# One joint region for two heads' last keys, another bank order, two store queues and new ranks in a planned attention-and-MLP kernel

## The chip, the cores and the metric

The kernel runs on one core of a Trainium2 chip. The metric is the device time of one launch in microseconds (us), lower being better. Before the change it is 1055.42 us, the median of 3 runs (1055.08 to 1056.28).

## The reference, cut to what matters

```python
q, k, v: [4, 8, 576, 64] fp32; tau: scalar
scores = (q @ k^T) / sqrt(64)
scores = where(scores >= rowmax - tau, scores, -1e9)
attn = exp(scores - rowmax); attn /= (rowsum + 1e-9)
x = (attn @ v) as [2304 tokens, 512]
h = x @ w_in;  x = (max(h, 0) + alpha * min(h, 0)) @ w_out     # d_ff = 2048
h = x @ w_in2; out = (h - tanh(h)) @ w_out2                    # d_ff = 2048
```

## The kernel before

The 2304 tokens are handled in 9 blocks of 256: two full blocks of each of the four batches (576 = 2 x 256 + 64), and one block made of the 64 left-over queries of all batches. Two heads are one attention unit, and a unit is visited in tiles of 128 queries. For a tile, TensorE forms the scores of both heads in PSUM (`multiply`, L700), VectorE takes the row maxima (`row_max`, L573) and the threshold (L576), ScalarE lifts the scores over the threshold and takes the exponential (`row_lift`, `row_exp`, L300 and L583), and VectorE the reciprocal of the sums. The first four units (`WHOLE = 4`) keep the exponentials as they are and turn them on TensorE, `turn_whole` the first 512 keys of a head and `turn_last` (L597) its last 64; copies on ScalarE or VectorE bring them into SBUF. Later units write two 16-bit pieces (`upper`, `lower`, L618) and turn them by DMA (L628). Products with the values are L739 and L742, later L679.

Every fp32 operand of the MLPs is split into a high and a low part, so one product is three matmuls. `turned_float` rounds weights as they arrive (`rebias` on ScalarE, L300 with `tw`; `three`, L367 or L369; `middle`, L372), `hi` copies (L297 or L295 inside `copy`) and `lo` subtracts (L303). The first MLP's first product is L915 (`h_pair`), its second L1140. In the second MLP, `out_products` sums seven smaller products by Strassen's scheme (`emit_seven`, L1032) for six of a block's eight pairs, and the plain product (`emit_plain`, L1039) for two of them, the last pair included. The sums lie in two PSUM tiles of two banks each, `sc0` and `sc1`. At the end of a block ScalarE copies one quarter out (`p1`), VectorE adds the rest (`total`, `both`, L1065), and the halves go to DRAM (`store`, L1085, and for the last block L1089).

The order of all this is no program text. `Plan.add` records each operation with the engines that may do it and an estimated time, its rank, what it reads and writes, and the PSUM banks and buffers it takes. `Plan.order` then walks through time: for each engine it takes, among the operations that could start first, the one of lowest rank, and among the engines the one that starts earliest after a penalty (`POOL_PEN`, `DVE_PEN`, `ACT_PEN`) where several could do it. The constants `TA`, `PA`, `PB`, `MLP_PE`, `MLP_G`, `PREP`, `XR` and the table `OFF` set the ranks. `N_WARM` operations of two matmuls on zeros (L1189), of the highest rank, fill TensorE where it has nothing else. Every engine then executes its own list strictly in that order, and DMAs stand in the lists of SyncE (SP) and ScalarE.

```python
add({"ACT": 0.49, "DVE": 0.62}, rank + OFF["H"], lambda e, j=j: bring(e, j), ...)   # ACT or DVE
t, r, i = min(((t, ops[i][1], i) for t, i in ests if t <= low + SLACK), key=lambda x: (x[1], x[2]))
key = (t + ((late_pen if ops[i][9] else pen)[e] if len(ops[i][0]) > 1 else 0), fin)
```

Of the kernel before, what the change touches and what calls it, by code (L numbers as in the profile page):

```python
# [9 lines left out]
F32 = mybir.dt.float32  # L10
# [14 lines left out]
P = 128  # L25
BLK = 256
NBLK = 9
# [17 lines left out]
TA = 69.2859  # L45
PA, PB = -14.922, 21.7041
MLP_PE = 1954.1131
MLP_G = -1037.3118
PREP = 2416.5189
# [7 lines left out]
POOL_PEN = 0.7718  # L57
# [7 lines left out]
XR = -5767.685  # L65
# [3 lines left out]
DVE_PEN = 0.5807  # L69
OFF = {"KS": -791.84, "S": -573.01, "M": -4327.05, "TH": -2173.26, "E": -1574.86, "X": -552.67, "R": -2860.41, "N": -5093.87, "NL": -258.85, "F": -1836.12, "DT": -6146.31, "T": 21.16, "H": 2659.35, "AV": -799.7, "XC": -548.69, "XH": -2968.53}  # L70
# [165 lines left out]
def attention_mlp_mlp(ctx: ExitStack, tc: tile.TileContext, kv, q0, q1, tau, w1i, w1o, alpha, w2i, w2o, out):  # L236
# [255 lines left out]
    def prep(u, rank):  # L492
# [8 lines left out]
        def load_qk(e):  # L501
            x = take(apool, raw, [P, 1024], F32, "rw", BUFS["rw"]) if u else T[raw]
            for a in range(2):
                e.dma_start(out=x[HALVES[a], :width], in_=packed_q[qb][b, h + a][HALVES[a]])
            if k == u > 0:
                load_k(e)

        def load_k(e):
            if not u:
                take(apool, raw, [P, 1024], F32, "rw", BUFS["rw"])  # L510
# [51 lines left out]
    def softmax(tile, n, slots, rank, eT, alone=False, w=False):  # L562
# [33 lines left out]
        def turn_last(e, j):  # L596
            e.transpose(hp[:D, j, :P], T["e", (tile, j)][:, 4 * P:], ident)  # L597
# [7 lines left out]
        def bring_last(e, j):  # L605
            copy(e, T[eT[eT[j][1]][0]][HALVES[j], 8 * P:], hp[:D, j, :P])
# [24 lines left out]
        for j, s in enumerate(slots):  # L631
            both = [("sc", s, t) for t in range(2)]
            k = add({"DVE": 0.69}, rank + OFF["M"], lambda e, j=j, s=s: row_max(e, j, s), [("sc", s, "s"), ROOM], [(*st, 0, j)], both,
                    takes=[] if j else [("st", st)], after=[k] if j else [])
        js = range(n)
        for a, b in [(j, j + 1) for j in js] if alone else [(0, n)]:
            add({"DVE": 0.15}, rank + OFF["TH"], lambda e, a=a, b=b: threshold(e, a, b), [*[(*st, 0, j) for j in range(a, b)], ("const", 0), ROOM],
# [7 lines left out]
        add({"DVE": 0.14}, rank + OFF["R"], guard, [*[(*st, 2, j) for j in js], ROOM], [(*st, 3)])  # L645
        add({"DVE": 0.08}, rank + OFF["R"], inverse, [ROOM], [(*st, 3)])
        k = None
        for j in js if w else ():
# [3 lines left out]
            add({"PE": 0.111}, rank + OFF["T"], lambda e, j=j: turn_last(e, j), [(*ej, 0), ("const", 2), ROOM], [("p5", j)], [("hp", 0)])  # L652
            begun[key] = add({"ACT": 0.49, "DVE": 0.62}, rank + OFF["H"], lambda e, j=j: bring(e, j), [("po", 0), ROOM], [(*key, at)], [("hp", 1)],
                             takes=[] if at else [("eT", key)], after=[begun[key]] if at else [])
        for j in js if w else ():
            key, at, _ = eT[j]
# [663 lines left out]
```

## Time and profile before

| what | value |
|---|---|
| median of 3 runs | 1055.42 us |
| the profiled execution's own time | 1052.59 us |
| span of its instructions | 1050.8 us |
| TensorE (PE) busy | 1023.7 us, 97%, 8859 matmuls |
| VectorE (DVE) busy | 772.9 us, 74% |
| ScalarE (ACT) busy | 618.4 us, 59% |
| GpSimd (POOL) busy | 74.4 us, 7% |

The span runs from the first to the last instruction on the core; the execution's own time is 1.8 us longer. The shares are means over stages that differ: until some 165 us ACT and DVE are busy about nine tenths of the time, later PE is busy nearly all the time. PE's busy time includes the 220 matmuls on zeros.

### The profile page before, as it was taken

How to read it: one execution, taken by the hardware profiler on the slowest of the kernel's cores; microseconds unless marked ns; L12 is line 12 of the kernel's file. 1: busy time of each engine (PE TensorE's matmuls, PEld its weight loads, DVE VectorE, ACT ScalarE, POOL GpSimd, SP SyncE). 2: the span in 40 equal slices, each digit the busy share in tenths (PEclk: the TensorE clock that was granted, in tenths of full speed). 3: DMA queues.
4: the chain of work that ended last, by engine and by line, in shares of the span. 5: the costliest groups of instructions: out<-in, count | busy, mean ns of one | idle time of the engine just before them, and what ended most of it. 6: DMA issues, size and time to landing. Idle time of an engine off the chain costs nothing.

```text
span 1050.8 us, 22486 instructions
## 1 busy us (share of the span) xinstructions
PE 1023.7 (97%) x8859; PEld 928.2 (88%) x8859; DVE 772.9 (74%) x1738; ACT 618.4 (59%) x1287; POOL 74.4 (7%) x101
## 2 busy tenths in 40 slices
PE   9979989999999999999999999999999999999997
PEld 7769879999999999998999888998898898899886
DVE  6998989878788778887857787674584484485465
ACT  6988888788788788887846554442312222331321
POOL 0122121001110111101100000000000000000000
PEclk9999999999999999999999999999999999999999
DMA  6678988758786557775585433200010010010000
GB/s 195 191 181 190 209 199 176 136 109 160 141 148 136 124 120 150 140 124 119 96 219 180 135 125 116 80 21 1 21 41 21 21 41 21 21 41 21 1 21 21
DMA packets 188890, 110.76 MB, mean 105 GB/s; under 512 B 158688, under 2 KB 171248, under 8 KB 188784
## 3 DMA queue, kind: packets, MB, share of 16 engines
q1 hardware_dynamic: 188480, 108.51, 44.8%
q8 instruction: 69, 1.13, 0.4%
q10 hardware_dynamic: 304, 0.82, 0.3%
q14 instruction: 37, 0.30, 0.1%
HBM read 61.58 MB, written 9.96 MB: 68 GB/s over the span
## 4 chain that ended last, share of the span: by engine, by line
PE 59%; DVE 2%; ACT 1%; DMA 1%; issue 1%; SPq 0%; DVEq 0%; ACTq 0%
PE sc L1032 13%; PE hp L915 10%; PE acc L869 6%; PE pt L915 5%; PE acc L1140 5%; PE sc L1039 5%; PE pt L869 3%; PE hp L869 3%; PE pt L679 2%; PE sc L1104 2%; PE acc L1104 2%; PE sc L700 1%; DVE st L573 1%; DMA eT<-rw 0%; ACT e L300 0%
## 5 line engine op out<-in xcount | busy, mean ns | idle before, releaser
L915 PE MATMUL hp<-x,i 128*128 128x256 f32 (+1 forms) x1584 | 230.9, 291 | 12.8 <-ACT e L300 5.6
L915 PEld LDWEIGHTS hp<-x,i 128*128 128x128 f32 x1584 | 206.1, 191 | 24.5 <-ACT e L300 6.1
L1140 PE MATMUL acc<-g,o 128*128 128x256 f32 x1232 | 165.7, 279 | 0.8 <-POOL g L303 0.8
L1140 PEld LDWEIGHTS acc<-g,o 128*128 128x128 f32 x1232 | 152.6, 188 | 4.4 <-POOL g L303 1.0
L300 ACT ACTIVATE e<-sc,st,qscale 128x576 f32<-128x576 f32 x144 | 118.0, 828 | 31.1 <-DVE st L576 18.9
L1032 PE MATMUL sc<-wp,g 128*128 128x256 f32 x756 | 135.8, 280 | 0.0
L1032 PEld LDWEIGHTS sc<-wp,g 128*128 128x128 f32 x756 | 115.8, 188 | 1.3
L618 DVE SCALAR_TENSOR_TENSOR rw<-e,st,rw 128x576 f16<-128x576 f32 x128 | 104.7, 835 | 10.3 <-ACT rw L295 9.7
L573 DVE TENSOR_REDUCE st<-sc 128x1 f32<-128x576 f32 x144 | 102.6, 750 | 13.1 <-PE sc L700 12.1
L583 ACT ACTIVATE e<-e,natau 128x576 f32<-128x576 f32 x144 | 110.9, 774 | 0.2
L1032 PE MATMUL sc<-wp,rw 128*128 128x256 f32 x378 | 106.1, 281 | 0.8 <-ACT o L295 0.8
L295 ACT ACTIVATE rw<-e,st 128x576 f16<-128x576 f32 x103 | 78.1, 771 | 18.3 <-DVE st L589 8.0
L295 ACT ACTIVATE g<-mr 128x512 fp32r<-128x512 f32 (+1 forms) x99 | 59.1, 597 | 47.8 <-PE sc L1104 16.7
L679 PE MATMUL pt<-eT,vs 128*64 128x256 f16 (+1 forms) x1584 | 73.3, 247 | 0.2 <-DMA eT<-rw 0.2
L1032 PEld LDWEIGHTS sc<-wp,rw 128*128 128x128 f32 x378 | 71.2, 188 | 2.3 <-ACT o L295 1.0
L303 DVE TENSOR_TENSOR g<-mr,g 128x512 fp32r<-128x512 f32 x80 | 55.6, 695 | 18.9 <-ACT g L295 18.4
L679 PEld LDWEIGHTS <-vs 128*64 128x64 bf16 x1584 | 65.0, 111 | 4.8 <-issue 0.4
L700 PE MATMUL sc<-kh,qh 64*128 64x320 f32 (+1 forms) x672 | 61.7, 310 | 4.4 <-ACT e L300 4.3
L869 PE MATMUL acc<-x,i 128*128 128x512 f32 x264 | 65.5, 395 | 0.0
L700 PEld LDWEIGHTS sc<-kh,qh 64*128 64x128 f32 x672 | 49.1, 185 | 13.2 <-ACT e L300 5.5
L869 PEld LDWEIGHTS acc<-x,i 128*128 128x128 f32 x264 | 48.9, 187 | 11.4
L915 PE MATMUL pt<-x,i 128*128 128x256 f32 (+1 forms) x352 | 58.0, 311 | 0.0
(246 smaller groups left out, 1707.4 us busy)
## 6 DMA issues: line engine op xcount, KB each, us to landing
vs<-in_kv_dram SPq DMA_DIRECT2D x58, 160.0 KB, 3.0
rw<-in_w1o_dram SPq DMA_DIRECT2D x16, 512.0 KB, 4.6
rw<-in_w2i_dram SPq DMA_DIRECT2D x16, 512.0 KB, 4.8
rw<-in_w2o_dram SPq DMA_DIRECT2D x16, 512.0 KB, 4.0
rw<-in_kv_dram SPq DMA_DIRECT2D x56, 144.0 KB, 3.0
rw<-in_w1i_dram SPq DMA_DIRECT2D x15, 512.0 KB, 4.8
out_dram<-o SPq DMA_DIRECT2D x16, 256.0 KB, 2.0
x1d<-o SPq DMA_DIRECT2D x14, 256.0 KB, 2.8
```

Of the source, the lines that this page charges most:

```text
L295: e.activation(out=out_, in_=in_, func=AF.Copy, **({} if scale is None else {"scale": scale}))
L300: e.activation(out=out_, in_=in_, func=AF.Prelu, alpha=alpha, **kw)
L303: e.tensor_tensor(out=out_, in0=in_, in1=hi.bitcast(F32), op=ALU.subtract)
L573: e.tensor_reduce(out=T[st][:, 0, j:j + 1], in_=x(s), axis=AX.X, op=ALU.max, negate=True)
L583: e.activation(out=w_, in_=w_, func=AF.Exp, bias=natau, scale=1.0, accum_out=T[st][:, 2, j:j + 1])
L618: e.scalar_tensor_tensor(out=x_[:, S + D:], in0=w_, scalar=r, in1=x_[:, :S], op0=ALU.mult, op1=ALU.subtract)
L679: e.matmul(po[HALVES[a]], lhsT=plane((k, a), part, c), rhs=eT(a, block), start=(i == 0), stop=(i == len(TERMS) - 1), skip_group_check=True)
L700: e.matmul(to(a, c), lhsT=x[HALVES[a], s], rhs=y[HALVES[a], c], start=(i == 0), stop=(i == len(terms) - 1))
L869: e.matmul(hq[k], lhsT=weight(1, "i", part, f // 4)[:, c, (f % 4) * P:(f % 4 + 1) * P], rhs=slots_of_x[x][:, :, c, :], start=(n0 + i == 0) ...
L915: e.matmul(hq if both_blocks else hq[:, k, :], lhsT=weight(l, "i", part, f // 4)[:, c, (f % 4) * P:(f % 4 + 1) * P], rhs=slots_of_x[x][:, ...
L1032: e.matmul(out_, lhsT=x[:, a], rhs=y[:, b], start=(begins and i == 0 and number in (1, 2, 5, 4)), stop=(n == NPAIR - 1 and i == 2), skip_g ...
L1140: e.matmul(acc[t][:, (c % 2) * BLK:(c % 2 + 1) * BLK], lhsT=w[:, c * P:(c + 1) * P], rhs=g[:, k, :], start=(f == 0 and n == 0 and c % 2 == ...
```

## The change

`turn_last` turns both heads' last keys of a tile into one region of 128 rows of PSUM (the second head by way of a 128-column transpose, the first one over its upper half), and `bring_last` brings them with one copy of 128 rows in place of two of 64. `emit_plain` and the final `both` and `store` take `sc1` ahead of `sc0`. The last block's four stores go out on two queues, two from SP and two from ACT. At the start the queries go out on SP ahead of tau, and the keys stand behind them in the plan. Some estimated times and all rank constants and two penalties have new values.

```diff
-TA = 69.2859
-PA, PB = -14.922, 21.7041
-MLP_PE = 1954.1131
-MLP_G = -1037.3118
-PREP = 2416.5189
+TA = 67.5119
+PA, PB = -68.347, 23.0966
+MLP_PE = 2066.0365
+MLP_G = -1104.8306
+PREP = 2493.5233
...
-POOL_PEN = 0.7718
+POOL_PEN = 0.5252
...
-DVE_PEN = 0.5807
+DVE_PEN = 0.5155
...
-            first = add({"ACT": 1.1}, -300, load_k, [ROOM], [(*raw, 1)], takes=[("rw", raw), ("qk", raw)], lag=3.0)
-            add({"SYNC": 2.5}, -300, load_qk, [ROOM], [raw], lag=DMA_LAG, after=[first])
+            first = add({"SYNC": 1.3}, -300, load_qk, [ROOM], [raw], takes=[("rw", raw), ("qk", raw)], lag=3.4)
+            add({"ACT": 1.1}, -300, load_k, [ROOM], [(*raw, 1)], lag=3.6, after=[first])
...
-        def turn_last(e, j):
-            e.transpose(hp[:D, j, :P], T["e", (tile, j)][:, 4 * P:], ident)
+        def turn_last(e):
+            e.transpose(hp[:, 0, :P], T["e", (tile, 1)][:, 4 * P - D:], ident)
+            e.transpose(hp[:D, 0, :P], T["e", (tile, 0)][:, 4 * P:], ident)
...
-        def bring_last(e, j):
-            copy(e, T[eT[eT[j][1]][0]][HALVES[j], 8 * P:], hp[:D, j, :P])
+        def bring_last(e):
+            copy(e, T[eT[eT[0][1]][0]][:, 8 * P:], hp[:, 0, :P])
...
-            for t in (1, 0):
+            for t in range(2):
                 for k in range(2):
                     x = 3 - 2 * t
...
-        for t in (1, 0):
+        for t in range(2):
             x = 3 - 2 * t
...
-            add({"SYNC": 1.2}, r, store, z, [("out", m, t)], lag=3.0)
+            if m < 2 * NBLK - 1:
+                add({"SYNC": 1.2}, r, store, z, [("out", m, t)], lag=3.0)
+            else:
+                add({"SYNC": 0.6}, r, lambda e, f=store: f(e, k=0), z, [("out", m, t, 0)], lag=2.0)
+                add({"ACT": 0.6}, r, lambda e, f=store: f(e, k=1), z, [("out", m, t, 1)], lag=2.0)
```

**ACT's list at the start, before** (`rw<-in_kv_dram` are the first unit's keys, `rw<-in_w1i_dram` the first piece of weights, `e<-sc` the first tile's `row_lift`):

```order
L512 DMA rw<-in_kv_dram 64x576 x2
L351 DMA rw<-in_w1i_dram 128x1024
L1183 ACT_TABLE_LOAD
L1183 ACTIVATE nalpha<-none 128x1
L300 ACTIVATE tw<-rw 128x512
L367 ACTIVATE rw<-rw 128x512
L300 ACTIVATE e<-sc_89,st,qscale 128x576
```

and now:

```order
L351 DMA rw<-in_w1i_dram 128x1024
L510 DMA rw<-in_kv_dram 64x576 x2
L1186 ACT_TABLE_LOAD
L1186 ACTIVATE nalpha<-none 128x1
L300 ACTIVATE tw<-rw 128x512 x2
L367 ACTIVATE rw<-rw 128x512
L295 ACTIVATE i_213<-tw 128x512
L300 ACTIVATE e<-sc_89,st,qscale 128x576
```

The first weights now go out ahead of the first keys, and four operations on weights stand ahead of the first tile's `row_lift` where there were two. On PE the transpose of alpha (`hp<-ident,o`) stood behind the first scores; it now stands ahead of them, with 30 matmuls on zeros before it and 8 behind it, where 36 stood ahead of the scores.

**POOL's list, its first operations behind the constants, before** (`rw<-rw` is `three`, `i`, `o`, `qh`, `last` are high or low parts):

```order
L369 TENSOR_SCALAR rw<-rw 128x512
L303 TENSOR_TENSOR o_414<-tw,o_414 128x512
L297 TENSOR_SCALAR last<-rw 64x64
L303 TENSOR_TENSOR last<-rw,last 64x64
L303 TENSOR_TENSOR qh<-rw,qh 128x256
L369 TENSOR_SCALAR rw<-rw 128x512
```

and now:

```order
L303 TENSOR_TENSOR o_390<-tw,o_390 128x512
L369 TENSOR_SCALAR rw<-rw 128x512 x2
L297 TENSOR_SCALAR o_390<-tw 128x512
L303 TENSOR_TENSOR o0b<-tw,o_390 128x512
L369 TENSOR_SCALAR rw<-rw 128x512
L303 TENSOR_TENSOR i_602<-tw,i_602 128x512
L297 TENSOR_SCALAR qh<-rw 128x256
L297 TENSOR_SCALAR last<-rw 64x64
```

More work on weights stands on POOL. Ahead of the 289th matmul of L915, where PE has 1532 matmuls behind it in either list, POOL has 49 instructions before and 78 now, DVE 355 and 321, ACT 277 and 272.

**DVE's list at the very end, before** (the last block's sums; `sc0` holds banks 0 and 1 of PSUM, `sc1` banks 2 and 3):

```order
L1065 TENSOR_TENSOR o_13522<-sc0_89,o_13522 128x256 [waits DMAHW0_49,PE_49,Activation_49]
L1065 TENSOR_TENSOR o_13521<-sc1_90,o_13522 128x256 [waits DMAHW1_49,DVE_49]
L1065 TENSOR_TENSOR o_13521<-sc1_90,o_13521 128x256 [waits DVE_49]
L1065 TENSOR_TENSOR o_13522<-sc1_90,o_13522 128x256
L1065 TENSOR_TENSOR o_13522<-sc0_89,o_13522 128x512 [waits DVE_49,PE_49]
L1065 TENSOR_TENSOR o_13521<-sc1_90,o_13521 128x512 [waits PE_49]
```

and now:

```order
L1064 TENSOR_TENSOR o_13514<-sc0_89,o_13514 128x256 [waits DMAHW0_49,Activation_49]
L1064 TENSOR_TENSOR o_13513<-sc1_90,o_13514 128x256 [waits DMAHW1_49,DVE_49,PE_49]
L1064 TENSOR_TENSOR o_13513<-sc1_90,o_13513 128x256 [waits DVE_49,PE_49]
L1064 TENSOR_TENSOR o_13514<-sc1_90,o_13514 128x256
L1064 TENSOR_TENSOR o_13513<-sc1_90,o_13513 128x512 [waits DVE_49]
L1064 TENSOR_TENSOR o_13514<-sc0_89,o_13514 128x512 [waits DVE_49,PE_49]
```

The first sum no longer waits for a plain matmul; the second now waits for the first three plain matmuls on `sc1`, the third for the next three. On PE, the twelve plain matmuls stood as three on `sc0` behind ACT's copy, three on `sc0` behind the first sum and six on `sc1` behind the fourth. Now they stand as three on `sc1` that wait for neither, three on `sc1` behind the second sum, and six on `sc0` behind ACT's copy.

## Rows read from the trace of the kernel before

**Rows 1.** The page's first part: busy time, share of the span and instructions by engine.

```profile
PE 1023.7 (97%) x8859; PEld 928.2 (88%) x8859; DVE 772.9 (74%) x1738; ACT 618.4 (59%) x1287; POOL 74.4 (7%) x101
```

**Rows 2.** Busy time by stretch: length, each engine's busy us and instructions, PE clock, DMA.

```profile
10.00:62.60 52.60, 52.60 (x468) 39.18 (x466) 48.87 (x117) 47.22 (x97) 7.71 (x10) 1.00 0.67 195
62.60:75.30 12.70, 5.77 (x45) 4.78 (x43) 12.34 (x29) 11.10 (x23) 4.65 (x5) 0.98 0.57 134
75.30:100.00 24.70, 24.70 (x265) 23.68 (x266) 22.22 (x48) 21.24 (x44) 2.46 (x5) 0.94 0.87 193
100.00:130.00 30.00, 26.64 (x292) 24.59 (x292) 28.06 (x59) 26.98 (x57) 6.36 (x7) 0.94 0.95 206
130.00:165.00 35.00, 30.17 (x348) 27.36 (x346) 31.80 (x67) 31.27 (x67) 8.97 (x9) 0.95 0.84 194
165.00:181.30 16.30, 16.30 (x173) 15.44 (x173) 14.61 (x34) 14.64 (x33) 1.89 (x3) 1.00 0.92 174
181.30:560.00 378.70, 374.47 (x4288) 356.84 (x4287) 305.91 (x670) 299.23 (x646) 40.62 (x54) 1.00 0.70 139
662.00:1041.00 379.00, 378.17 (x2443) 343.04 (x2442) 228.47 (x570) 111.64 (x233) 0.00 (x0) 1.00 0.07 25
```

**Rows 3.** Timeline of the first 12 us: start, us, engine, line, tiles, idle before.

```profile
0.73 1.20 ACTq L512 DMA_DIRECT2D rw<-in_kv_dram  x2
1.97 0.71 ACTq L351 DMA_DIRECT2D rw<-in_w1i_dram  x1
2.45 0.58 SPq L1185 DMA_DIRECT2D o<-in_alpha_dram  x1
3.08 1.57 SPq L351 DMA_DIRECT2D rw<-in_w1i_dram  x2
...
0.99 6.79 PE L1189 MATMUL acc<-none 128*128 128x256 bf16 x36 [0.99 <-POOL none L1177]
7.72 1.57 PE L700 MATMUL sc<-rw 64*128 64x320 f32 x8
9.22 0.69 ACT L300 ACTIVATE tw<-rw 128x512 f32<-128x512 f32 x1 [5.01 <-DMA rw<-in_w1i_dram]
9.78 0.67 ACT L367 ACTIVATE rw<-rw 128x512 int32<-128x512 uint32 x1
10.84 1.56 ACT L300 ACTIVATE e<-sc,st,qscale 128x576 f32<-128x576 f32 x2 [0.38 <-DVE st L576]
```

**Rows 4.** DMA issues of the first 12 us: KB each, median us from issue to landing.

```profile
rw<-in_w1i_dram SPq DMA_DIRECT2D x2, 512.0 KB, 7.2
rw<-in_w1i_dram ACTq DMA_DIRECT2D x1, 512.0 KB, 7.2
o<-in_alpha_dram SPq DMA_DIRECT2D x1, 8.0 KB, 5.8
rw<-in_kv_dram ACTq DMA_DIRECT2D x2, 144.0 KB, 3.8
```

**Rows 5.** The chain that ended last, its end: start, us, engine and line.

```profile
1041.32 0.39 ACT o L295
1041.75 0.97 PE sc L1039 x3
1042.81 0.43 DVE o L1065
1043.72 0.77 DVE o L1065 x2
1044.54 1.68 PE sc L1039 x6
1046.23 0.69 DVE o L1065
```

**Rows 6.** Timeline from 1045.96 us on SP: the last three stores.

```profile
1045.96 2.10 SPq L1089 DMA_DIRECT2D out_dram<-o  x3
```

**Rows 7.** `lower` on DVE: all of it on the page, and one beside POOL in the timeline.

```profile
L618 DVE SCALAR_TENSOR_TENSOR rw<-e,st,rw 128x576 f16<-128x576 f32 x128 | 104.7, 835 | 10.3 <-ACT rw L295 9.7
...
160.87 2.78 POOL L552 TENSOR_TENSOR vs<-vs 128x320 f32<-128x320 f32 x2 [4.12 <-DMA vs<-in_kv_dram]
161.79 1.28 DVE L618 SCALAR_TENSOR_TENSOR rw<-e,st,rw 128x576 f16<-128x576 f32 x1
```

More of the change, by code (lines that the diff above doesn't have):

```diff
@@ L501, in load_qk @@
         def load_qk(e):
-            x = take(apool, raw, [P, 1024], F32, "rw", BUFS["rw"]) if u else T[raw]
+            x = take(apool, raw, [P, 1024], F32, "rw", BUFS["rw"])
             for a in range(2):
@@ L632, in softmax @@
             both = [("sc", s, t) for t in range(2)]
[L633 removed]
+            k = add({"DVE": 0.67}, rank + OFF["M"], lambda e, j=j, s=s: row_max(e, j, s), [("sc", s, "s"), ROOM], [(*st, 0, j)], both,
                     takes=[] if j else [("st", st)], after=[k] if j else [])
@@ L636, in softmax @@
         for a, b in [(j, j + 1) for j in js] if alone else [(0, n)]:
-            add({"DVE": 0.15}, rank + OFF["TH"], lambda e, a=a, b=b: threshold(e, a, b), [*[(*st, 0, j) for j in range(a, b)], ("const", 0), ROOM],
+            add({"DVE": 0.19}, rank + OFF["TH"], lambda e, a=a, b=b: threshold(e, a, b), [*[(*st, 0, j) for j in range(a, b)], ("const", 0), ROOM],
                 [(*st, 1, j) for j in range(a, b)])
@@ L644, in softmax @@
             add({"ACT": 0.76}, rank + OFF["X"], lambda e, j=j: row_exp(e, j), [("const", 0), ROOM], [(*ej, 0), (*st, 2, j)])
-        add({"DVE": 0.14}, rank + OFF["R"], guard, [*[(*st, 2, j) for j in js], ROOM], [(*st, 3)])
+        add({"DVE": 0.075}, rank + OFF["R"], guard, [*[(*st, 2, j) for j in js], ROOM], [(*st, 3)])
         add({"DVE": 0.08}, rank + OFF["R"], inverse, [ROOM], [(*st, 3)])
@@ L651, in softmax @@
             add({"PE": 0.438}, rank + OFF["T"], lambda e, j=j: turn_whole(e, j), [(*ej, 0), ("const", 2), ROOM], [("po", 0), ("po", 1)], [("hp", 1)])
-            add({"PE": 0.111}, rank + OFF["T"], lambda e, j=j: turn_last(e, j), [(*ej, 0), ("const", 2), ROOM], [("p5", j)], [("hp", 0)])
             begun[key] = add({"ACT": 0.49, "DVE": 0.62}, rank + OFF["H"], lambda e, j=j: bring(e, j), [("po", 0), ROOM], [(*key, at)], [("hp", 1)],
                              takes=[] if at else [("eT", key)], after=[begun[key]] if at else [])
-        for j in js if w else ():
-            key, at, _ = eT[j]
-            add({"ACT": 0.19, "DVE": 0.2}, rank + OFF["H"], lambda e, j=j: bring_last(e, j), [("p5", j), ROOM], [(*eT[at][0], 5, j)], [("hp", 0)], after=[begun[eT[at][0]]])
+        if w:
+            to = eT[eT[0][1]][0]
+            add({"PE": 0.22}, rank + OFF["T"], turn_last, [*[("e", (tile, j), 0) for j in js], ("const", 2), ROOM], [("p5", 0)], [("hp", 0)])
+            add({"ACT": 0.29, "DVE": 0.28}, rank + OFF["H"], bring_last, [("p5", 0), ROOM], [(*to, 5, j) for j in js], [("hp", 0)], after=[begun[to]])
         for j in js if not w else ():
@@ L1080, in both, with store @@
                 total(e, T[o[t]], two_banks(x), T[o[t]])
-            def store(e, t=t):
+            def store(e, t=t, k=None):
                 if m < 2 * NBLK - 1:
@@ L1086, in store @@
                 else:
-                    for k in range(2):
+                    for k in (k,):
                         row = (2 * t + k + 1) * S - D
```

6 lines of the change are left out of this document (2 added, 4 removed).

## The prediction

> **What bounds the kernel now.** I read the page's totals first, then the busy time by stretch, since the totals mix stages. PE is busy 97% of the span [rows 1], but the stretches tell of two kernels. From 181.3 us to 560 us PE has 4.2 us of idle time (378.70 less 374.47), from 662 to 1041 us 0.8 us [rows 2]: there PE sets the pace, and whatever is done to another engine moves nothing that can be counted. From 10 to 181.3 us it is otherwise. DVE is busy 157.9 of 171.3 us there (the sum of its first six stretches), ACT 152.5 us, so 92% and 89%; PE's 100% before 62.6 us is filled up with matmuls on zeros. From 62.6 to 165 us PE idles 15.1 us (6.93, then 3.36 and 4.83) and gets a granted clock of 0.94 to 0.95, that is some tenth of the time at 1.2 instead of 2.4 GHz, in stretches that lie in or right behind that idle time [rows 2]. So before 181 us the pace is set by DVE and ACT together, and the time lost there is never made good, because PE has no slack behind it. The third place is the end: the chain that ended last goes back and forth between ACT, PE and DVE for five microseconds, with nothing else running [rows 5]. These three places, start, first 181 us and end, are where the change can count.
>
> **The end.** Today ACT's copy starts at 1041.32 us and takes 0.39, the first three plain matmuls wait for it and take 0.97, the first sum starts at 1042.81, 0.09 us behind them, and so on in single file to the last sum, which ends at 1046.92 [rows 5]. With the new order the first three plain matmuls run beside the copy, on the other PSUM tile, and are over at some 1042.2. The first sum needs the copy alone: 1041.71 plus 0.09 plus 0.43 is 1042.23. The second sum follows at once, to 1042.7. The second three matmuls start at 1042.75, and the six others follow in the stream: six more matmuls beyond three cost 6 x 0.237 us (the difference of 1.68 and 0.97, by three), so all nine are done at 1042.75 + 0.97 + 1.42 = 1045.14. The third and fourth sums need the second three, at 1043.72, and take 0.77: 1044.6. The two joint sums of 0.69 then end at 1045.3 and 1046.05 [rows 5]. That is 0.87 us earlier. Behind the last sum stand two stores one after the other on SP: from 1046.92 to the end of the last three issues, 1045.96 + 2.10 = 1048.06, are 1.14 us, so 0.57 each [rows 6]. Now each queue has one; ACT's issues take about the same, two in 1.20 [rows 3]. That takes off another 0.57. The end gives **-1.4 us**. Its bounds are 0 (ACT's queue adds what the order saves) and -1.9 (the matmuls beside the copy cost nothing at all). The same swap in the other seven plain places changes nothing: PE has 0.8 us of idle time in that whole stretch [rows 2].
>
> **The start.** The first scores start at 7.72 us behind 36 matmuls on zeros, and the first row lift at 10.84, 0.38 us after ACT went idle [rows 3]. The change puts alpha's transpose ahead of the scores. Alpha is issued at 2.45 and lands 5.8 us later [rows 3, 4], so at 8.25; its place in SP's list hardly moves. Eight matmuls on zeros behind it, at 0.19 us each (6.79 by 36, rows 3) or less, put the scores at about 9.5. The keys, now behind 512 KB of weights on ACT's queue, need not come sooner. The row lift has to wait for more: ACT's list has the third piece of weights ahead of it. That one is the second of the two issues on SP that start at 3.08, so it is issued towards 4.3 and lands 7.2 us after [rows 3, 4], at 11.5. Then come L367 with 0.67 and a copy of the same size, taken at 0.67 too, so 12.85 instead of 10.84: 2.0 us later. Ahead of it ACT has by then done two more weight operations, worth 1.35 us, that it need not do later. Net **+0.7 us** on ACT; bounds 0 (ACT's later idle time swallows it) and +2.0. Tau one place later in the list costs nothing: it is needed only for the threshold ahead of the row lift, at 10.84.
>
> **The first 181 us.** I take as a mark the 289th matmul of L915, at 181.3 us, because PE has the same 1532 matmuls behind it in both lists. DVE has 34 fewer instructions ahead of it (355 and 321), ACT 5 fewer (277 and 272), POOL 29 more (49 and 78), as counted in the lists. Among DVE's are five half-height copies that the joint region saves (ten of 64 rows become five of 128); ACT's saving from it is three of six. At the mean of a DVE instruction in these stretches, 157.9 us by 354 or 0.446, DVE is rid of 15.2 us; ACT, at 152.5 by 321 or 0.475, of 2.4; POOL, at 32.0 by 39 or 0.82, gets 23.8 more [rows 2]. This is the crux, for what POOL does is not free to DVE. `lower` takes 0.835 us on DVE on average, and 1.28 us where it ran beside two POOL subtractions [rows 7]: it stood still for 0.45 us. Call s the part of POOL's added time that DVE loses. No row gives s for a list with more on POOL, so I bound it by 0 (everything lies beside reductions out of PSUM) and 1. I take one half, nearest to that one row, where DVE lost 0.45 us of the 1.28 in which both ran. DVE then gains 15.2 - 11.9 = 3.3 us, ACT 2.4 less the 0.7 of the start, which is 1.7. Both set the pace, so the stretch shortens by the lesser: **-2.4** for ACT's list, with the +0.7 above. Beyond the mark PE is full, and I take nothing. I also take the granted clock as it is. It can go either way by as much as the idle time does: a tenth of the 90 us from 75.3 to 165 ran at the low clock [rows 2], so at most some 5 us are in it.
>
> **Sum.** -1.4 + 0.7 - 2.4 = -3.1 us. The profiled execution took 1052.59 us (a span of 1050.8 and 1.8 around it), which makes 1049.5. The median of the three runs stands 2.8 us above that execution, at 1055.42, so I say **1052.3 us**, 0.3% less. About 0.2% (2.1 us) is what a measurement of this kernel tells from no change. The forecast's own range, with the bounds of end and start and s from 0.4 to 0.65, is 1050 to 1054.5.
>
> **The rivals.** *POOL's work falls beside PSUM work* (faster still). If s is 0.2, DVE loses 4.8 of the 15.2 us, keeps 10.4, and the waits of ACT and PE on DVE go with it. If half of PE's 15.1 us of idle time [rows 2] goes, the kernel gains 7.5 + 1.4 = 8.9: 1046.5. For it: DVE is the busier of the two engines. Against it: ACT stays at 89%, and the new list of POOL has weight splits right at its front, where DVE runs the same kind of work.
>
> *POOL holds DVE up* (slower). Above s = 0.64 DVE loses more than it is rid of, and from s = 0.78 on (23.8 s - 15.2 - 1.4 above 2.1) the kernel is slower by more than 0.2%. At s = 0.9 the stretch grows by 6.2 us, and the kernel is at 1055.4 + 6.2 - 1.4 = 1060.2. The place is 10 to 181 us, on DVE's instructions with two operands in SBUF: L618, L372 and L303. For it: the 1.28 us of rows 7, and that DVE has only 8% of idle time to give. Against it: POOL's present 32 us go along with a DVE that is 92% busy. The Trainium skill has a rule for this, in SBUF — State Buffer, "Who interferes with whom": a VectorE instruction with two SBUF inputs contends with a GpSimd instruction that reads SBUF, and the second to issue is blocked until the first is done. By that rule the sum is this rival's wherever such pairs meet. The one `lower` of rows 7 agrees with it, with 0.45 us.
>
> *The late start is passed on whole.* If the scores behind alpha and the weights ahead of the keys delay DVE as well as ACT, 2.0 us go through undiminished, and the shorter lists are eaten up by waits: +2.0 - 1.4 = +0.6, 1056.0. For it: both engines are full right behind the start. Against it: the operations that were moved ahead are then no longer to be done.
>
> *The end doesn't do what it says.* If ACT's queue stores later than SP would, or the new waits on PE cost as much as the old, the end gives nothing, and -1.7 remains: 1053.7, no measurable change.
>
> **How the numbers follow.** The forecast has 0.40 (0.30 of it faster by over 0.2%, 0.10 within), POOL beside PSUM 0.17, POOL holding DVE 0.20, the start passed on 0.15 (0.12 within, 0.03 slower), the end without gain 0.08. So faster 0.47, within 0.2% 0.30, slower 0.23. The range reaches from a little below the fast rival to the price of the slow one: 1046 to 1060.5.
>
> **What would show it.** In the chain of the changed kernel the first sum should start at about 1041.8 less whatever the front saved, with a single store of each queue behind the last sum. The first row lift should stand near 12.9 us. POOL should be busy some 50 to 60 us more in all, and the mean of `lower` on DVE should tell s: near 0.84 us for the fast rival, above 0.95 for the slow one. PE's idle time from 62 to 165 us should be 13 to 14 us. The forecast is wrong if the 289th matmul of L915 comes later than 181.3 us, or if PE gets new idle time behind it, where I allow none.

## The result, and the profile after

The changed kernel takes 1064.97 us (median of 6 runs, 1063.22 to 1066.33); the kernel before took 1054.04 us in its runs beside it. The ratio is 1.0102, with a 95% interval of 1.0083 to 1.0121: some 10.8 us slower. That is outside the stated range, and on the other side of the forecast. The profiled execution has a span of 1064.5 us, 13.7 us more than the one of before; the two executions lie on opposite sides of their medians, so for the size the ratio counts, and the profiles for the places.

Where the 13.7 us of the two profiles lie is read off at three marks of TensorE: the first and the last of the seven-sum matmuls of the second MLP (`sc<-wp,rw` and `sc<-wp,g`), and the end of the span. The middle column runs from the start of the first to the end of the last.

| | first MLP ends (first seven-sum matmul) | from there to the last of them | from there to the end of the span | span |
|---|---|---|---|---|
| before | 662.25 | 379.03 | 9.52 | 1050.8 |
| after | 671.13 | 384.84 | 8.55 | 1064.5 |
| difference | +8.9 | +5.8 | -1.0 | +13.7 |

The end does what was forecast, if not to the full. The other two are losses in stretches where I had allowed none. The profiled execution is the slowest of the six, and that shows in the first MLP: three of the runs below (plain_back, plain_x_back, x_on_dve) have the same order there and end it at 667.45, 668.19 and 668.54 us. So 5 to 6 of the 8.9 us recur, and the rest belongs to this execution.

**Totals and stretches.** The page's first part, and the busy time by stretch (columns as in [rows 2]):

```profile
PE 1032.6 (97%) x8859; PEld 932.8 (88%) x8859; DVE 763.3 (72%) x1672; ACT 609.6 (57%) x1272; POOL 138.1 (13%) x174
```

```profile
62.60:75.30 12.70, 8.02 (x66) 6.57 (x66) 10.41 (x24) 11.49 (x27) 5.62 (x7) 1.00 0.38 98
75.30:120.00 44.70, 38.70 (x413) 37.18 (x414) 39.27 (x82) 36.99 (x81) 13.37 (x16) 0.85 0.87 189
120.00:165.00 45.00, 41.89 (x468) 38.55 (x467) 42.31 (x80) 36.30 (x75) 18.29 (x18) 0.96 0.88 198
181.30:560.00 378.70, 373.35 (x4234) 352.85 (x4234) 297.88 (x630) 289.55 (x630) 72.33 (x98) 1.00 0.69 133
662.00:1041.00 379.00, 375.34 (x2387) 336.76 (x2386) 220.88 (x550) 112.94 (x237) 7.18 (x3) 1.00 0.07 26
```

POOL has 63.7 us more [rows 1], a little over the forecast 50 to 60. DVE has 66 instructions less, but only 9.6 us less of busy time. PE's idle time from 62.6 to 165 us is 13.8 us (4.68, 6.00, 3.11), as forecast, yet the granted clock is 1.00, 0.85 and 0.96 there where it was 0.94 to 0.98 [rows 2]. By those rows 0.15 x 44.7 + 0.04 x 45, or 8.5 us' worth of clock, was lost (17.1 us at the lower of its two levels), 5.3 before. The 289th matmul of the first product (L914, before L915) comes at 183.98 us, 2.7 later. And from 181.3 to 560 us, where I called PE full, it is 1.1 us less busy than before, but the first MLP falls another 6 us behind. Busy time does not show this: a matmul of this kind is booked with 0.28 us from its start while the next mostly starts 0.11 us later (medians of both traces), so a wait of up to 0.17 us leaves no gap.

**The start.** The timeline of the first 13 us, by engine (columns as in [rows 3]):

```profile
7.64 0.20 PE L1189 MATMUL hp<-ident,o 16*128 16x16 f32 x1 [1.14 <-DMA o<-in_alpha_dram]
7.77 1.05 PE L1192 MATMUL acc<-none 128*128 128x256 bf16 x8
8.75 1.24 PE L699 MATMUL sc<-rw 64*128 64x320 f32 x8
...
10.02 1.42 DVE L571 TENSOR_REDUCE st<-sc 128x1 f32<-128x576 f32 x2 [1.14 <-PE sc L699]
11.36 0.68 DVE L372 SCALAR_TENSOR_TENSOR tw<-tw,rw 128x512 int32<-128x512 int32 x1
11.96 0.28 DVE L574 TENSOR_SCALAR st<-st,qscale,atau 128x2 f32<-128x2 f32 x1
...
11.12 0.69 ACT L367 ACTIVATE rw<-rw 128x512 int32<-128x512 uint32 x1 [1.98 <-DMA rw<-in_w1i_dram]
12.08 0.63 ACT L295 ACTIVATE i<-tw 128x512 fp32r<-128x512 f32 x1 [0.26 <-DVE tw L372]
12.61 1.54 ACT L300 ACTIVATE e<-sc,st,qscale 128x576 f32<-128x576 f32 x2
```

The row lift starts at 12.61 us (forecast 12.85, before 10.84), and what held it last is what was forecast: ACT waits until 11.12 for the third piece of weights, and the lift follows the copy that its list has ahead of it. Nearly as late comes another chain that was not in that sum: eight matmuls on zeros stand between alpha's transposition and the scores, and a weight operation (L372) ahead of the threshold, which ends at 12.24.

**A plain pair of the second MLP.** The timeline of PE, DVE and POOL around 770 us:

```profile
769.21 0.96 PE L1038 MATMUL sc<-wp,g 128*128 128x512 f32 x3
770.69 2.33 PE L1038 MATMUL sc<-wp,g 128*128 128x512 f32 x9 [0.52 <-DVE o L1064]
...
768.27 0.88 DVE L1064 TENSOR_TENSOR o<-sc,o 128x256 f32<-128x256 f32 x2
770.21 0.42 DVE L1064 TENSOR_TENSOR o<-sc,o 128x256 f32<-128x256 f32 x1 [1.06 <-PE sc L1038]
771.69 0.69 DVE L1064 TENSOR_TENSOR o<-sc,o 128x512 f32<-128x512 f32 x1 [0.46 <-PE sc L1038]
772.30 1.12 DVE L979 TENSOR_TENSOR gs<-mr 128x128 f32<-128x128 f32 x1
...
770.87 2.39 POOL L303 TENSOR_TENSOR x<-rw,x 128x1024 fp32r<-128x1024 f32 x1 [230.14 <-ACT x L295]
```

The first plain matmuls of a new block now write `sc1`, while DVE's sums of the block before still have to read `sc1`. So the third sum waits 1.06 us for PE, PE's next nine wait 0.52 us for that sum, and the next sum waits again. Of the 18 plain pairs four meet this: they take 3.65 us from the first matmul to what follows, the others, but for the very last, 2.73 to 2.79. The subtraction of 128x1024 is new on POOL, and beside it a DVE operation of 0.28 us takes 1.12.

**VectorE beside POOL.** One `guard` (L584) with POOL's subtraction next to it:

```profile
401.42 1.43 POOL L303 TENSOR_TENSOR kh<-rw,kh 128x576 fp32r<-128x576 f32 x1
...
401.52 1.35 DVE L584 TENSOR_SCALAR st<-st 128x2 f32<-128x2 f32 x1 [0.15 <-ACT e L581]
402.91 0.17 DVE L587 RECIPROCAL st<-st 128x2 f32<-128x2 f32 x1
```

The guard, 0.16 us where it runs alone, ends 26 ns behind POOL's instruction, and so do all 20 guards that take over 0.23 us here (22 to 30 ns behind; 9 of them before). The groups of DVE's instructions by form (count, busy us and mean ns), threshold and guard before:

```profile
L576 DVE TENSOR_SCALAR st<-st,qscale,atau 128x2 f32<-128x2 f32 x64 | 18.3, 285 | 0.1
L586 DVE TENSOR_SCALAR st<-st 128x2 f32<-128x2 f32 x64 | 14.4, 225 | 21.5 <-ACT e L583 21.3
```

and now:

```profile
L617 DVE SCALAR_TENSOR_TENSOR rw<-e,st,rw 128x576 f16<-128x576 f32 x128 | 104.5, 832 | 12.3 <-ACT rw L295 11.2
L574 DVE TENSOR_SCALAR st<-st,qscale,atau 128x2 f32<-128x2 f32 x64 | 22.7, 355 | 0.2
L584 DVE TENSOR_SCALAR st<-st 128x2 f32<-128x2 f32 x64 | 21.4, 334 | 25.2 <-ACT e L581 25.2
L584 DVE TENSOR_SCALAR st<-st 128x1 f32<-128x1 f32 x16 | 2.3, 147 | 0.4 <-ACT e L581 0.3
L587 DVE RECIPROCAL st<-st 128x2 f32<-128x2 f32 x64 | 10.3, 162 | 1.2
```

`lower` (L617), the one I watched, has the mean of before. Guard of two columns has 334 ns (225 before), threshold 355 (285); guard of one column and the reciprocal are as ever. If what an instruction takes beside POOL over the median of its own line, operation and tiles without POOL counts as lost, DVE lost 10.5 us before and loses 29.7 now (10.4 and 28.7 where different shapes are kept apart too).

**The end.** The chain that ended last, its end; then the timeline of the stores; then their issues (KB each, median us to landing):

```profile
1056.01 0.39 ACT o L295
...
1056.42 0.44 DVE o L1064
...
1056.94 0.44 DVE o L1064
...
1057.42 0.98 PE sc L1038 x3
...
1058.42 1.37 DVE o L1064 x3
...
1059.80 0.69 DVE o L1064
```

```profile
1059.80 1.25 SPq L1088 DMA_DIRECT2D out_dram<-o  x2
1059.81 1.45 ACTq L1088 DMA_DIRECT2D out_dram<-o  x2
```

```profile
out_dram<-o SPq DMA_DIRECT2D x2, 128.0 KB, 2.4
out_dram<-o ACTq DMA_DIRECT2D x2, 128.0 KB, 2.8
```

From ACT's copy to the last sum's end are 4.48 us, where [rows 5] give 5.60: 1.1 us gained. From the last sum to the end of the span are 4.0 us, 3.9 before: the second queue gives nothing. Its issues end 0.4 us sooner behind the last sum than SP's four did, and land later. How late varies: in the profiles of plain_back and plain_x_back below, with the same end, ACT's two land 3.2 us behind their issue.

### The profile page after: what moved, and what is told of

The parts are those of the page before. It is cut to its first block, busy times and chain, and to the rows that moved or that the text cites. A ratio compares the mean times of both kernels' runs of the same rounds, so it can differ in the third digit from the quotient of the medians.

```text
span 1064.5 us, 22541 instructions
## 1 busy us (share of the span) xinstructions
PE 1032.6 (97%) x8859; PEld 932.8 (88%) x8859; DVE 763.3 (72%) x1672; ACT 609.6 (57%) x1272; POOL 138.1 (13%) x174
## 4 chain that ended last, share of the span: by engine, by line
PE 48%; DVE 3%; ACT 1%; issue 0%; DMA 0%; SPq 0%; ACTq 0%; DVEq 0%
PE sc L1031 12%; PE hp L914 7%; PE acc L868 6%; PE pt L914 5%; PE sc L1038 4%; PE pt L868 3%; PE hp L868 3%; PE acc L1143 2%; PE sc L1107 2%; PE acc L1107 2%; DVE o L1064 1%; PE pt L678 1%; DVE gs L979 0%; DVE rw L617 0%; ACT e L300 0%
## 5 line engine op out<-in xcount | busy, mean ns | idle before, releaser
L914 PE MATMUL hp<-x,i 128*128 128x256 f32 (+1 forms) x1584 | 231.9, 292 | 12.7 <-DVE mr L935 10.7
L914 PEld LDWEIGHTS hp<-x,i 128*128 128x128 f32 x1584 | 207.1, 192 | 24.0 <-issue 5.5
L300 ACT ACTIVATE e<-sc,st,qscale 128x576 f32<-128x576 f32 x144 | 115.5, 824 | 17.5 <-DVE st L587 9.3
L617 DVE SCALAR_TENSOR_TENSOR rw<-e,st,rw 128x576 f16<-128x576 f32 x128 | 104.5, 832 | 12.3 <-ACT rw L295 11.2
L295 ACT ACTIVATE rw<-e,st 128x576 f16<-128x576 f32 x100 | 75.5, 771 | 37.5 <-issue 10.5
L303 DVE TENSOR_TENSOR g<-mr,g 128x512 fp32r<-128x512 f32 x80 | 57.2, 714 | 24.7 <-ACT g L295 24.4
L699 PE MATMUL sc<-kh,qh 64*128 64x320 f32 (+1 forms) x672 | 65.7, 317 | 1.7 <-ACT e L300 1.1
L699 PEld LDWEIGHTS sc<-kh,qh 64*128 64x128 f32 x672 | 52.0, 189 | 11.9 <-issue 2.7
L935 DVE SCALAR_TENSOR_TENSOR mr<-mr,nalpha,hp 128x256 f32<-128x256 f32 x112 | 49.5, 474 | 13.7 <-ACT mr L928 13.4
L303 POOL TENSOR_TENSOR x<-rw,x 128x1024 fp32r<-128x1024 f32 x3 | 7.2, 2394 | 400.1 <-ACT x L295 400.1
```

Of the source, the lines that this page charges most:

```text
L295: e.activation(out=out_, in_=in_, func=AF.Copy, **({} if scale is None else {"scale": scale}))
L300: e.activation(out=out_, in_=in_, func=AF.Prelu, alpha=alpha, **kw)
L303: e.tensor_tensor(out=out_, in0=in_, in1=hi.bitcast(F32), op=ALU.subtract)
L617: e.scalar_tensor_tensor(out=x_[:, S + D:], in0=w_, scalar=r, in1=x_[:, :S], op0=ALU.mult, op1=ALU.subtract)
L699: e.matmul(to(a, c), lhsT=x[HALVES[a], s], rhs=y[HALVES[a], c], start=(i == 0), stop=(i == len(terms) - 1))
L914: e.matmul(hq if both_blocks else hq[:, k, :], lhsT=weight(l, "i", part, f // 4)[:, c, (f % 4) * P:(f % 4 + 1) * P], rhs=slots_of_x[x][:, ...
```

## The experiments

Theory at the outset: the second MLP's loss comes from the bank order; the first MLP's from POOL holding DVE up, let in by the new estimate of guard (the planner keeps POOL and a DVE operation apart only where that is put over 0.1 us) and by the lower penalties. Rivals: POOL's wide subtraction for the one, the new order as such for the other.

**The bank order (plain_back).**

```diff
-            for t in range(2):
+            for t in range(2) if p == 2 * NBLK * NPAIR - 1 else (1, 0):
                 for k in range(2):
...
-        for t in range(2):
+        for t in range(2) if m == 2 * NBLK - 1 else (1, 0):
             x = 3 - 2 * t
```

> The changed kernel with the plain pairs and their last sums in the old bank order (sc0 first), except for the very last pair; the order of everything ahead of the second MLP is the same. Theory: after the change four plain pairs take 3.65 us instead of 2.75 and what follows each is late by another 0.5, because their first matmuls write sc1 while the sums of the block before still have to read it; 4 x 1.45 us = 5.8 us come back: 1065.0 - 5.8 = 1059.2 us, all plain pairs but the last at 2.73 to 2.79 us. Rival: in three of the four places a 2.4 us subtraction on POOL is new and holds VectorE up, and the order of banks costs nothing: 1065 us, the four pairs stay at 3.65.

Measured: 1062.44 us, ratio 1.0085 (1.0062 to 1.0108). All plain pairs but the last are back at 2.73 to 2.76 us, but from the first to the last seven-sum matmul are 382.38 us: 2.5 come back, not 5.8. At three places something else is late now (timeline of DVE and POOL):

```profile
767.53 2.19 DVE L979 TENSOR_TENSOR gs<-mr 128x128 f32<-128x128 f32 x1
...
767.16 2.41 POOL L303 TENSOR_TENSOR x<-rw,x 128x1024 fp32r<-128x1024 f32 x1 [230.12 <-ACT x L295]
```

Both theory and rival have a part in it.

**The wide subtraction (plain_x_back and x_on_dve).** The first is plain_back, the second the changed kernel, each with

```diff
-        add({"DVE": 1.14, "POOL": 2.4}, rank, lo, [raw] + [("x0", m, c) for c in range(4)], [("x1", m, c) for c in range(4)])
+        add({"DVE": 1.14}, rank, lo, [raw] + [("x0", m, c) for c in range(4)], [("x1", m, c) for c in range(4)])
```

> The run with the old bank order, and besides the 128x1024 subtraction of the second MLP's inputs kept on VectorE. In that run all plain pairs but the last were back at 2.75 us, but each of the three places with that subtraction on POOL still lost 1.1 us, as VectorE's sums of 128x128 beside it waited some 1.9 us. Theory: both together cause the second MLP's loss, and hide each other; without either the first and the last of its seven-sum matmuls lie 379.0 us apart as before the change (384.8 after it, 382.4 with the old bank order alone), and the time is 1062.4 - 3.3 = 1059.1 us. Rival: POOL's subtraction only fills idle time, something else of the new order is late: 382.4 stays.

> The changed kernel with that subtraction on VectorE, but with the new bank order. If bank order and subtraction hide each other, each of the four places loses what the fourth, which has no such subtraction, lost after the change, 1.27 us: first and last seven-sum matmul lie 379.0 + 5.1 = 384.1 us apart (384.8 after the change). If the subtraction alone were the cause of the three, 379.0 + 1.3 = 380.3.

Measured: plain_x_back 1058.09 us, 1.0040 (1.0025 to 1.0054), and 379.03 us between the two marks, to the hundredth what it was before the change. x_on_dve, a single run of 1062.50 us, has 383.63 us there, four pairs at 3.65. So the bank order alone costs 4.6 us, the subtraction alone 3.3, both together 5.8: they hide each other. With the order gone, the same place as above:

```profile
766.07 2.91 PE L1038 MATMUL sc<-wp,g 128*128 128x512 f32 x12
...
767.66 0.69 DVE L1064 TENSOR_TENSOR o<-sc,o 128x512 f32<-128x512 f32 x1
768.27 0.28 DVE L979 TENSOR_TENSOR gs<-mr 128x128 f32<-128x128 f32 x1
```

The second MLP is settled by this. What is left, 1.0040 with the end's gain in it (in this profile 0.3 us, not 1.0), is the first MLP.

**More work on POOL, nothing else (pool_load).**

```diff
+        warm_left = N_WARM
...
                 plan.ops[i][2](engine[e])
+                warm_left -= plan.ops[i][1] == 1e9
+                if e == "POOL" and not warm_left:
+                    for _ in range(2):
+                        nc.gpsimd.tensor_tensor(out=none, in0=none, in1=none, op=ALU.subtract)
```

> The kernel before, with the order on all engines unchanged, and behind each of POOL's operations from the last matmul on zeros on two subtractions of 128x128 in SBUF of 0.35 us that nobody needs: about 60 us more on POOL, as the change adds. Theory: VectorE loses at least 20 us beside POOL instead of 10.5, and the kernel takes 3 to 6 us more: 1057 to 1060. Rival: VectorE has room for it, the time stays within 1.5 us of 1054.0.

Measured: 1060.01 us, 1.0057 (1.0041 to 1.0073). Page, first part, and a stretch:

```profile
PE 1027.9 (97%) x8859; PEld 930.6 (88%) x8859; DVE 786.3 (74%) x1738; ACT 617.5 (58%) x1287; POOL 158.7 (15%) x271
```

```profile
181.30:560.00 378.70, 371.85 (x4245) 353.02 (x4245) 309.07 (x661) 296.32 (x643) 96.52 (x168) 1.00 0.70 136
662.00:1041.00 379.00, 378.17 (x2425) 342.19 (x2424) 228.13 (x568) 112.83 (x235) 0.00 (x0) 1.00 0.07 26
```

POOL got 84 us, more than meant. DVE's busy time rose by 13.4 us for no work (lost beside POOL 24.5 us, 10.5 before), and the first MLP ended 7.4 us later, 4.9 of them between the 181.3 us mark and its end, where PE had been called full. So POOL's work does cost, and there too.

**The standing still turned into work (stallers_dve, all_dve).** The order is kept; HOLDS are the numbers of the 46 operations (for all_dve the condition is that DVE may do it):

```diff
+        n_pool = -1
...
+                if e == "POOL" and len(plan.ops[i][0]) > 1:
+                    n_pool += 1
+                    if n_pool in HOLDS:
+                        e = "DVE"
                 plan.ops[i][2](engine[e])
```

> The changed kernel, all orders kept, but 46 operations of the first MLP beside which VectorE lost over 0.15 us go to VectorE, at their places in the order, instead of POOL. VectorE gets 25 us of work and is rid of 25 us of standing still. Theory: standing still is dearer than work, since it falls on guards and thresholds that ScalarE and TensorE wait for at once: 2 to 4 us less, 1061 to 1063 us. Rival: VectorE's busy time in sum decides: 1065 within 1.5.

> The same for all of POOL's 166 operations that VectorE may do: no standing still at all, but some 62 us of work more on VectorE, 38 net. If POOL's help is worth what it costs, this is slower than the changed kernel by 5 us or more (1070); if contention is the dearer, it is faster than 1065.

Measured: stallers_dve 1063.56 us, 1.0098 (1.0075 to 1.0121); all_dve 1080.87 us, 1.0260 (1.0242 to 1.0277). In stallers_dve DVE loses 7.5 us beside POOL instead of 29.7, and its busy time is 761.2 us instead of 763.3: the trade was even, and the time is that of the changed kernel within the intervals. Standing still is not dearer than work; the theory falls here. Nor does contention, taken in sum, account for what is left of the first MLP's loss: DVE stands still less here than before the change (10.5 us) and is less busy (772.9 us), and the first seven-sum matmul still comes at 667.18 us. all_dve shows that POOL's help is worth having.

**The constants undone one group at a time (guard_port, pens_back, ranks_back), and the estimates alone on the kernel before (estimates_only).**

```diff
-        add({"DVE": 0.075}, rank + OFF["R"], guard, [*[(*st, 2, j) for j in js], ROOM], [(*st, 3)])
+        add({"DVE": 0.14}, rank + OFF["R"], guard, [*[(*st, 2, j) for j in js], ROOM], [(*st, 3)])
...
-POOL_PEN = 0.5252
+POOL_PEN = 0.7718
...
-DVE_PEN = 0.5155
+DVE_PEN = 0.5807
```

> The changed kernel with the estimate of guard at 0.14 us as before, instead of 0.075. The planner keeps POOL and a VectorE operation apart only where the latter is put at more than 0.1 us. Theory: with 0.075 it lets POOL run beside guard, and guard then ends some 25 ns after POOL's instruction: 20 guards of over 0.23 us, 11.0 us lost in guard alone and 29.7 us in all VectorE instructions beside POOL (9 guards, 3.9 and 10.5 us before the change). With 0.14 guard's share falls under 5 us, and some 3 us of the 8.9 us that the first MLP is late come back: 1062 us. Rival: the new ranks as such give the late order, contention only fills time in which VectorE waits anyway: guard's share falls, and the time stays at 1065 within 1.5.

> The changed kernel with the two old penalties (POOL 0.7718, VectorE 0.5807), new ranks. Theory: POOL's busy time falls from 138 us to about 85, the time that VectorE loses beside it from 29.7 to about 15 us, and some 4 us come back: 1061 us. Rival (the ranks as such): POOL's share falls, and the time stays at 1065 within 1.5 or rises, since the ranks were made for the new penalties.

> The changed kernel with all old ranks and both old penalties; joint region, start, bank order and estimates stay. If the new ranks are what makes the first MLP late, its end comes back to within 2 us of before (the second MLP's first sum at 661 to 664 us instead of 667.5 to 671), and the second MLP's loss by bank order stays: 1058. If the first MLP's lateness comes from the other parts, or any order that was not tried out on the chip is late by some us, it stays at 667 us or later: 1063 or more.

> The kernel before with only the three new estimates (row_max 0.67, threshold 0.19, guard 0.075), old ranks, old penalties: the planner gives another order. If any order that is planned anew from these ranks is late, this is 5 to 20 us later than 1054 like the others (pens_back, guard_port and ranks_back lie 18 to 25 us behind it). If the estimates are harmless, it stays within 2 us of 1054.

Measured: guard_port 1079.13 us, 1.0229 (1.0207 to 1.0251); pens_back 1072.2, 1.0181 (1.0161 to 1.0202); ranks_back 1073.12, 1.0177 (1.0161 to 1.0192); estimates_only 1067.91, 1.0137 (1.0122 to 1.0152). guard_port is the first pair of lines of the diff, pens_back the other two; ranks_back takes back the penalties and all rank constants as in the change's diff; estimates_only puts the three estimates into the kernel before. Every one is slower than its starting point, by 7 to 15 us. Each of these edits makes the planner order the whole first MLP anew. In guard_port, for example, PE and its clock fall off in one stretch:

```profile
120.00:165.00 45.00, 30.76 (x327) 26.18 (x326) 35.46 (x69) 36.46 (x76) 11.73 (x16) 0.77 0.87 189
```

And guard still loses 11.5 us beside POOL there (pens_back: 12.7), so the planner's 0.1 us limit is not what lets POOL in: that step of the theory is wrong as well. These four runs say nothing on contention. They say that ranks, penalties and estimates fit only as a set.

**The parts at the old order (start_fixed, joint_fixed, tail_only, parts_old_order).** The instructions of each part are changed, the planner's order stays. The edits in brief:

```diff
+        keys = order.pop(first("ACT", -300))
+        order.insert(first("ACT", -200) + 1, keys)
+        queries = order.pop(first("SYNC", -300))
+        order.insert(0, queries)
...
+        turned = order.pop(first("PE", -250))
...
+        order.insert(scores, turned)
...
-            e.transpose(hp[:D, j, :P], T["e", (tile, j)][:, 4 * P:], ident)
+            seen[0] += 1
+            if seen[0] == 2:
+                e.transpose(hp[:, 0, :P], T["e", (tile, 1)][:, 4 * P - D:], ident)
+                e.transpose(hp[:D, 0, :P], T["e", (tile, 0)][:, 4 * P:], ident)
...
-            for t in (1, 0):
+            for t in range(2) if p == 2 * NBLK * NPAIR - 1 else (1, 0):
```

> The kernel before with its own order, and only the start of the change: queries ahead of tau on SP, the first keys behind the first weights on ScalarE's queue, alpha's transposition ahead of the first scores. Theory: the first scores come about 1 us later, and since ScalarE and VectorE are nine tenths busy behind it, the second MLP's first sum comes later by about as much, 1 to 1.5 us (663.3 to 663.8 us in the profile): 1055 to 1055.5. Rival: idle time swallows it, 1054.0 within 0.5.

> The kernel before with its own order, and only the joint region: both transpositions where the second stood, one copy of 128 rows in place of two of 64, at the first place where both heads are turned. Theory: 8 copies of 0.2 to 0.28 us less, in the first 62 us, and nothing waits longer: the first product of the first MLP up to 1 us sooner, 1053 to 1054. Rival: waiting for both heads costs more than the copies save, 1055 or more, and the joint region is what makes the changed kernel's first MLP late.

> The kernel before with its own order, and only the end of the change: the very last plain pair and its last sums by the other bank first, the last block's stores on two queues. After the change the last sum came 1.1 us sooner behind the last of the seven-sum matmuls than before, and the span ended 1.0 us sooner, so the second queue gave nothing. Theory: 9.5 us from there to the end of the span become 8.5, 1053.0 us. By the forecast it would be 8.1 us and 1052.6.

> The kernel before with its own order and all of the change's parts that bind only their own place: joint region, start and end. Theory: the parts cost and gain what they did alone (1.0004, 1.0004, 0.9991), so 1054.0 within 1 us, and the second MLP's first sum stands at 661 to 665 us; the 6 us of the first MLP lie in the order alone. Rival: together they bind one another, 1056 or more.

Measured: start_fixed 1.0004 (0.9991 to 1.0018), joint_fixed 1.0004 (0.9995 to 1.0014), tail_only 0.9991 (0.9982 to 1.0001), all three together 0.9997 (0.9985 to 1.0009; 1053.89 us). In start_fixed the first scores come at 7.56 us, no later than the 7.72 of [rows 3], since alpha landed in time and no matmuls on zeros stand in between. In tail_only the end of the span lies 8.5 us behind the last seven-sum matmul, as expected by theory. In the profiles of parts_old_order and joint_fixed the first seven-sum matmul comes at 665.19 us (expected 661 to 665) and 665.13, 3 us behind the profile before, but the ratio of joint_fixed leaves the joint region at most 1.5 us. So by the times none of these parts makes the first MLP late by more than that.

**What can be mended in the new order (start_mend, mended, plain_x_start, before_mended).** start_mend moves the first scores ahead of the eight matmuls on zeros, and the first threshold and row lifts ahead of the weight operations:

```diff
+        order.insert(at("PE", -250) + 1, order.pop(at("PE", OFF["S"])))
+        for k, (e, name) in enumerate((("DVE", "TH"), ("ACT", "E"), ("ACT", "E"))):
+            order.insert(at("DVE", OFF["M"], 1) + 1 + k, order.pop(at(e, OFF[name], max(0, k - 1))))
```

> The changed kernel, its order kept but for four operations at the start: the first scores right behind alpha's transposition, the first threshold and the two first row lifts right behind the row maxima. Theory: the first row lift starts at 10.8 us as before instead of 12.6, TensorE is 1.5 to 1.8 us further on at 60 us, and since ScalarE and VectorE are full behind it, that stays to the end: 1065.0 - 1.6 = 1063.4. Rival: idle time further on swallows it, 1065.

> All cures together: the start as in start_mend, the 46 operations on VectorE, plain pairs in the old bank order but for the last, the wide subtraction on VectorE. Theory: 1065.0 less 6.9 (the run with the second MLP mended) less 1.6 (start) less 1 (standing still) = 1055.5, and what is then left beside the kernel with the new end alone, 2 us, is what the rest of the new order costs in the first MLP. Rival: the cures don't add up, since what one gives back the next wait takes: 1058.

> The changed kernel with the second MLP mended (old bank order but for the last pair, wide subtraction on VectorE) and the four operations at the start moved ahead. If the start's 1.8 us pass through, 1058.1 - 1.8 = 1056.3. If TensorE's first 60 us swallow them, as the profile of start_mend shows it (the first product of the first MLP no sooner than after the change), 1058.1 within 0.7.

> The kernel before with the new end (last pair and last sums, two queues) and 21 operations beside which VectorE lost over 0.15 us on VectorE instead of POOL. Theory: 1.0 us from the end, and 0 to 1.5 us from 9 us of standing still turned into some 11 us of work: 1052 to 1053.3, the fastest so far. Rival: VectorE is the fuller engine here and pays: 1054 or more.

Measured: start_mend 1061.4 us, 1.0075 (1.0062 to 1.0088). Its timeline of ACT and PE:

```profile
10.78 1.55 ACT L300 ACTIVATE e<-sc,st,qscale 128x576 f32<-128x576 f32 x2 [1.73 <-DVE st L574]
...
68.80 1.20 PE L914 MATMUL hp<-x,i 128*128 128x256 f32 x9
```

The row lift is back at 10.78 us, but the first product of the first MLP starts at 68.80 us (67.63 after the change, 62.62 before). The 1.8 us are gone by then, so the gain in the time, twice what was expected, has another source, or is chance: the first MLP ends at 666.42 us here, 1.0 us before the earliest of the four executions with this first MLP that are named under the result. Where the second MLP is mended, the same four moves bring nothing: plain_x_start 1.0046 (1.0033 to 1.0060), plain_x_back 1.0040. mended, with all cures, is at 1.0044 (1.0027 to 1.0060): beyond the second MLP's the cures bring nothing. before_mended is at 0.9998 (0.9988 to 1.0008). No version clearly beats the kernel before; tail_only comes nearest, and its interval reaches past 1.

## Why the prediction was wrong

**The end: right, with one term mis-sized.** The bank order gave 1.1 us (forecast 0.87), the second queue nothing (forecast 0.57). I took ACT's issue for as good as SP's; behind the issue the landing is 2.8 us instead of 2.4. Together -1.0 for -1.4, inside the bounds.

**"The same swap in the other seven plain places changes nothing": the first step that failed.** There are 17 other plain pairs, not seven, and four of them lost by it. The argument was that PE has only 0.8 us of idle time in that stretch, so there is nothing to gain. But a stage that is full has nothing to win and everything to lose. The swap puts PE's first writes into the tile that DVE still reads, and I had seen that at the end, where it was a gain, but did not ask who still reads `sc1` when the next block's first plain pair begins. It cost 4.6 us alone (x_on_dve).

**"Beyond the mark PE is full, and I take nothing": the second.** It failed twice. Three subtractions that went to POOL in the second MLP have time to spare themselves; what they hold up is not their reader, it is DVE's 128x128 operations beside them: 3.3 us alone (plain_back). And PE's busy share hid the first MLP's sensitivity: pool_load, with nothing changed but idle work on POOL, lost 4.9 us beyond the mark while PE's busy time there fell by 2.6.

**The first 181 us.** The counts were right, the part s was not: over the whole kernel POOL got 63.7 us and DVE lost 19.2 more, so s is 0.30, up to the mark 0.28 (7.7 of 27.5 us), and 0.16 in pool_load (13.4 of 84.3 us). I took 0.5 from the one `lower` of [rows 7], but that row has 0.45 us lost beside 2.78 us of POOL's work, which is 0.16, and even of DVE's 1.28 us it is 0.35. So DVE did become freer, as the fast rival has it: 9.6 us less busy in sum. From 10 us to the mark, before and after:

```profile
10.00:181.30 171.30, 156.19 (x1579) 135.03 (x1577) 157.88 (x349) 152.46 (x316) 32.04 (x38) 0.97 0.80 190
10.00:183.98 173.98, 158.72 (x1581) 138.27 (x1581) 151.51 (x311) 147.03 (x308) 59.51 (x67) 0.95 0.76 184
```

DVE is busy 6.4 us less and ACT 5.4, more than the forecast 3.3 and 1.7, and the time did not follow. The mark came 2.7 us later. PE is idle as long as before (15.3 us, 15.1); it is busy 2.5 us longer, and the low clock took up to 3.2 us more there; I had left the clock as it is. In plain_back, with the same order, the clock was low for 10.2 us up to the mark, as long as before the change, and the mark came at 182.26 us. So some 1.0 of the 2.7 us is there without more of the low clock, and the rest goes with it. The step that failed is that the stretch shortens with the sum of the work on the engine that is busiest. parts_old_order and plain_x_back say what does count: with the old order the parts give 0.9997, with the new order and the second MLP mended 1.0040, some 4.5 us (1.7 to 7.3 by the ends of the two intervals, and 0.7 of it in the profiles' last stores). By elimination (start, joint region and end cost next to nothing at the old order; an even trade of standing still for work changes nothing) this is the price of the new order of the first MLP; by what wait it is paid, no run shows. Which of its places costs how much I could not settle: the waits of PE there are many and short, and the one place that I could name, the start, was not it.

**The rivals.** "POOL holds DVE up" had the right sign and mechanism, and for the most part the wrong place: of the 29.7 us 12.0 fall before the mark (4.3 before the change), and 4.1 of these on L618, L372 and L303; guard, threshold and the 128x128 sums lose most, all along. By stallers_dve it does not explain the first MLP. The Trainium skill's page SBUF — State Buffer, "Who interferes with whom", says more than I drew from it: it lists `tensor_scalar` too among the VectorE operations that can take the shared ports, where their operands meet the conditions of the modes with two ports, and says that the later one waits until the other is over. The trace agrees to 30 ns for the guards of two columns. By the sum I weighed only the operations with two inputs. "The late start is passed on whole" was not borne out: with the start moved back the first product came no sooner (68.80 us for 67.63), and plain_x_start gained nothing on plain_x_back.

**The size of the range.** 1046 to 1060.5 held no case in which two stretches lose that I had called full. plain_x_back, which is the change without the second MLP's loss, would have been inside it.

## What to carry to other kernels

A full stage is the place to look for losses, not the place to skip: for every store or matmul that is moved there, ask which engine still reads that tile, and for every operation put on another engine, what runs beside it. Busy time of an engine whose instructions overlap hides short waits; compare the start of the same matmul in both traces instead. And where a planner makes the order, its ranks, penalties and estimates hold only as a set: judge a part of a change with the order held fixed, for the order made anew can cost more than every part together.

## What the runs showed of the hardware that was not expected

A VectorE `tensor_scalar` of 128x2, 0.16 us alone, stood still for up to 1.2 us beside a GpSimd instruction and ended 22 to 30 ns behind it; the same operation on 128x1 kept its 147 ns, and the reciprocal on 128x2 its 162. The same order of the first MLP ran at the lower TensorE clock for 10 to 20 us of its first 181 us, from run to run (10.2 in plain_back, 17.1 in after and plain_x_back, 20.5 in x_on_dve, by the granted clock's record), and its 289th matmul came at 182.3, 184.0, 183.2 and 184.8 us.
